# Mirrored rows read in 15 and 112 instead of 127, and the last batch's fold one MLP step later

## The chip, the cores and the metric

The kernel runs on one core of one Trainium2 chip. The metric is the device time of one execution in microseconds (us). Before the change three executions took 962.08, 965.52 and 968.96 us; their median is 965.52 us.

## The reference: what is computed

Three layers stand one behind the other, on 4 batches of 576 positions and 512 features.

```python
scores = scale * np.matmul(q, k.transpose(0, 1, 3, 2))     # 8 heads, local or strided mask
attn_out = softmax(masked scores) @ v                      # becomes x, [4, 576, 512]
...
X = np.fft.fft(np.fft.fft(x, axis=1), axis=2)
u = x + np.real(X)
un = (u - mean(u)) / np.sqrt(var(u) + 1e-06)
x = u + np.maximum(un @ w_ch1, 0.0) @ w_ch2                # first MLP, hidden width 2048
...
u = x + token_mlp(x)                                       # over the 576 positions
out = u + np.maximum(u @ w_ch1, 0.0) @ w_ch2               # second MLP, hidden width 1536
```

The change lies where the attention's result x of a batch is read for the Fourier layer.

## The kernel before, in words

**Stages.** Attention of the four batches comes first: per batch three groups of local heads and three of strided heads (matrix products `sc` for the scores, softmax on ScalarE, transposes `tp`, products `av`). The result `x` of each group is written to a DRAM buffer `xd[b]` (lines 270, 276, 277). The Fourier layer of batch b is worked off between the attention groups of later batches (`four[b]`), that of the last batch, `four[3]`, inside the first MLP. Then come the first MLP, the token layer and the second MLP.

**The Fourier layer of a batch.** The real part of a 2-D transform of real data is symmetric, so rows r and 576 - r are added first. `load(i)` (i = 0, 1, 2; 128, 128 and 33 rows) reads rows r0 and following of `xd[b]` into a tile `xa`, and the rows that mirror them into a tile `xr`; the second half of the positions is stored in reverse, so that the mirrored rows are consecutive too. For i = 0 row 0 has no mirror: row 0 of `xr` is set to zero on GpSimd, and the read brings rows 1 to 127, which are 127 rows of 2 KB (line 297). `prep(i)` (lines 299 to 316) folds on VectorE: `w` = xa + xr, then the two halves of `e`; ScalarE rounds `e` to `f` (line 315), GpSimd takes the rest (line 316). `s1(mt)`, five of them, multiplies `f` with the constants (products `g`, line 332), and ScalarE and VectorE split the result into `gh` and `gl` (lines 340, 342; `g4h`, `g4l` for the fifth). `s2(i)` multiplies these with further constants (products `fa`, `fb`, line 358), ScalarE copies `fa` to `sa`, VectorE forms `m` (lines 365, 366), adds it to `xa` and `xr` (line 371), and both are stored to `ud[b]` (lines 373, 374).

**The first MLP.** A step (c, f) takes one chunk c of 384 rows and one block f of 128 hidden units: 12 products `h` (line 411), the split of `h` into `hh` (ScalarE, line 415) and `hl` (VectorE, line 416), 9 products `oo` (line 430). `last_fft(x)` is called in the first nine steps and hands out the pieces of `four[3]`: the folds in steps 1 to 3, the `s1` in 3 to 5, the `s2` in 6 and 7, and in step 8 the memory of the Fourier constants is given to weights. Every step also begins to load one weight block: transfer `wraw` (line 101), four VectorE operations on `wu` (lines 108 to 113), `wAh` on ScalarE, `wAl` on GpSimd.

**What sets the order.** A scheduler orders the instructions of each engine at build time by its own model of time; `behind` gives it single orders (VectorE's fold behind an `hl` or a reduction `st`). On the chip each engine works through its list in that order, and an instruction that waits holds all behind it. SyncE (SP) issues all the transfers named here, in one list. Transfers that SP issues are given eight completion semaphores in turn, so a transfer can be issued only when the eighth before it has landed.

```python
self.last = nc.sync.dma_start(out=xr[z:n], in_=xd[self.b][287 + r0 + z:287 + r0 + n, :])
```

Of the kernel before, what the change touches and what calls it, by code (L numbers as in the profile page):

```python
# [43 lines left out]
def attention_fourier_mlp_kernel(ctx: ExitStack, tc: tile.TileContext, a: dict, out: bass.AP):  # L44
    nc = tc.nc
# [16 lines left out]
    xd = [dram.tile([S, DM], F32, name=f"xd{b}") for b in range(B)]  # L62
# [218 lines left out]
    class Fourier:  # L281
# [4 lines left out]
        def load(self, i):  # L286
            r0, n = ST[i]
            pool = self.pool if self.b % 2 else self.k["pool"]
            xa, xr = (pool.tile([P, DM], F32, tag=f"{x}{i}", name=x, bufs=1) for x in ("xa", "xr"))
            self.x[i] = xa, xr  # L290
            na, z = min(n, 288 - r0), 1 if i == 0 else 0
            if i == 2:
                nc.gpsimd.memset(xa[32:33], 0.0)
            if i == 0:
                nc.gpsimd.memset(xr[0:1], 0.0)
            nc.sync.dma_start(out=xa[:na], in_=xd[self.b][r0:r0 + na, :])
            self.last = nc.sync.dma_start(out=xr[z:n], in_=xd[self.b][287 + r0 + z:287 + r0 + n, :])

        def prep(self, i, prev=None, prev2=None):
            r0, n = ST[i]  # L300
# [187 lines left out]
    if True:  # L488
# [144 lines left out]
        def last_fft(x):  # L633
            nonlocal wb, wc
            x4 = four[3]
            prev = relu["hh"], relu["hl"]
            if 1 <= x < 4:
                x4.prep(x - 1, prev[1], prev[0])
            x4.after = prev
            for mt in {3: (0,), 4: (1, 2), 5: (3, 4)}.get(x, ()):  # L640
                x4.s1(mt)
            for i in {6: (0,), 7: (1, 2)}.get(x, ()):
                x4.s2(i)
            if x == 8:
                fst.close()
                wb = wbst.enter_context(tc.tile_pool(name="wb", bufs=16, side="left", reuse_waits="tile"))
                wc = wcst.enter_context(tc.tile_pool(name="wc", bufs=16, side="left", reuse_waits="tile"))
# [100 lines left out]
        def extra1(c, f):  # L748
            if steps.index((c, f)) <= 8:
                last_fft(steps.index((c, f)))  # L750
            advance()
            load_wa()
            if 2 <= c < NCH - 1 and f % 4 == 1:
                m, h = divmod((c - 2) * 4 + f // 4, 2)
                begin(blocks("2", m, 128 * h))
            if 2 <= c < NCH - 1 and f % 4 == 3:
                m, h = divmod((c - 2) * 4 + f // 4, 2)
                begin(blocks("1", m, 128 * h))
            if c == NCH - 1:
                if f >= 1:  # L760
                    load_wt()
                if f == 2:
                    c_load(0, range(3), 3)
                if f == 9:
                    c_load(1, range(5), 3)
# [458 lines left out]
```

## Time and profile before

| what | value |
|---|---|
| median of three executions | 965.52 us (962.08 to 968.96) |
| the profiled execution's own time | 963.61 us |
| its span, first to last instruction | 961.7 us |
| TensorE busy in the span | 900.6 us, 94% |
| VectorE, ScalarE, GpSimd busy | 559.4, 409.0, 307.7 us |
| mean granted TensorE clock | 0.976 of full |
| bytes moved by DMA | 160.99 MB, mean 167 GB/s |

The span is cut into views: what each engine waited for, the order of work on one engine (timeline), busy time in chosen stretches with the granted clock (1.00 is 2.4 GHz, 0.50 is 1.2 GHz) and the share of time in which the 16 DMA engines were busy, and the chain of work that ended last. "A <- B" in a wait says that A began when B ended. All rows are of the profiled execution, so sums are made against its 963.61 us.

### The profile page before, as it was taken

How to read it: one execution, taken by the hardware profiler on the slowest of the kernel's cores; microseconds unless marked ns; L12 is line 12 of the kernel's file. 1: busy time of each engine (PE TensorE's matmuls, PEld its weight loads, DVE VectorE, ACT ScalarE, POOL GpSimd, SP SyncE). 2: the span in 40 equal slices, each digit the busy share in tenths (PEclk: the TensorE clock that was granted, in tenths of full speed). 3: DMA queues.
4: the chain of work that ended last, by engine and by line, in shares of the span. 5: the costliest groups of instructions: out<-in, count | busy, mean ns of one | idle time of the engine just before them, and what ended most of it. 6: DMA issues, size and time to landing. Idle time of an engine off the chain costs nothing.

```text
span 961.7 us, 15392 instructions
## 1 busy us (share of the span) xinstructions
PE 900.6 (94%) x5554; PEld 830.6 (86%) x5554; DVE 559.4 (58%) x1046; ACT 409.0 (43%) x1069; POOL 307.7 (32%) x372
## 2 busy tenths in 40 slices
PE   7949688699999999999999999999999999999997
PEld 6949587589889899989788898777799999999997
DVE  4636677488999444343333344753725353989774
ACT  6948465345334224324222222521446454634441
POOL 4211212123333013434344344440430301746751
PEclk9979797999999999999999999999999999999999
DMA  9966654233443134465465565668943358344451
GB/s 253 270 206 200 201 175 149 94 124 113 137 134 108 66 111 136 125 190 152 141 186 151 150 208 161 181 209 284 351 166 153 129 184 278 89 149 164 171 197 45
DMA packets 116852, 160.99 MB, mean 167 GB/s; under 512 B 9543, under 2 KB 70061, under 8 KB 116777
## 3 DMA queue, kind: packets, MB, share of 16 engines
q1 hardware_dynamic: 114808, 157.29, 51.9%
q0 software_dynamic: 1712, 2.51, 1.0%
q8 instruction: 44, 0.72, 0.3%
q14 instruction: 32, 0.25, 0.1%
q10 hardware_dynamic: 256, 0.21, 0.1%
HBM read 104.92 MB, written 55.06 MB: 166 GB/s over the span
## 4 chain that ended last, share of the span: by engine, by line
PE 51%; DMA 19%; DVE 14%; SPq 5%; issue 4%; ACT 4%; POOL 4%; DVEq 0%; ACTq 0%; POOLq 0%
PE oo L1034 14%; PE z L893 8%; PE oo L430 6%; DMA xr<-xd 6%; PE h L411 5%; DMA wraw<-in_w1b_dram 5%; PE y L893 4%; SPq L101 3%; DMA xd<-x 3%; PE tu L804 3%; PE tk L782 3%; DVE wu L113 3%; DVE wu L112 3%; POOL wt L147 2%; DMA wraw<-in_w2b_dram 2%
## 5 line engine op out<-in xcount | busy, mean ns | idle before, releaser
L411 PE MATMUL h<-uT,wAh 128*128 128x384 f32 x768 | 203.0, 338 | 0.2
L411 PEld LDWEIGHTS h<-uT,wAh 128*128 128x128 f32 x768 | 139.1, 188 | 5.2 <-PE g L332 0.4
L1034 PE MATMUL oo<-wo,ht 128*128 128x256 f32 x972 | 133.7, 281 | 0.0
L411 PE MATMUL h<-uT,wAl 128*128 128x384 f32 x384 | 129.2, 336 | 0.0
L1034 PEld LDWEIGHTS oo<-wo,ht 128*128 128x128 f32 x972 | 126.5, 189 | 0.0
L430 PE MATMUL oo<-wAh,hh 128*128 128x512 f32 x288 | 114.2, 399 | 8.0 <-ACT hh L415 7.2
L430 PE MATMUL oo<-wAl,hh 128*128 128x512 f32 x288 | 113.6, 394 | 0.0
L430 PE MATMUL oo<-wAh,hl 128*128 128x512 f32 x288 | 105.3, 396 | 0.7 <-DVE hl L416 0.7
L416 DVE SCALAR_TENSOR_TENSOR hl<-h,hh 128x384 fp32r<-128x384 f32 x96 | 52.5, 552 | 74.9 <-ACT hh L415 74.9
L108 DVE TENSOR_SCALAR wu<-wu 128x512 f32<-128x512 f32 (+1 forms) x62 | 35.0, 565 | 85.5 <-ACT wu L106 79.4
L124 POOL TENSOR_TENSOR wAl<-wu,wAh 128x512 fp32r<-128x512 f32 x32 | 43.2, 1352 | 102.1 <-ACT wAh L123 100.7
L411 PEld LDWEIGHTS h<-uT,wAl 128*128 128x128 f32 x384 | 72.3, 188 | 3.0
L147 POOL TENSOR_TENSOR wt<-wu 128x128 f32<-128x128 f32 x48 | 21.1, 461 | 161.9 <-DVE wu L113 161.9
L106 ACT ACTIVATE wu<-wraw 128x512 f32<-128x512 f32 (+1 forms) x62 | 41.2, 664 | 72.8 <-DMA wraw<-in_w1b_dram 50.6
L430 PEld LDWEIGHTS oo<-wAh,hh 128*128 128x128 f32 x288 | 54.1, 188 | 20.4 <-ACT hh L415 9.8
L415 ACT ACTIVATE hh<-h 128x384 fp32r<-128x384 f32 x96 | 45.6, 481 | 53.2 <-PE h L411 50.8
L430 PEld LDWEIGHTS oo<-wAh,hl 128*128 128x128 f32 x288 | 53.6, 188 | 15.0 <-DVE hl L416 2.8
L893 PE MATMUL z<-ut,wo 128*128 128x384 f32 x324 | 64.5, 338 | 1.7 <-DVE ut L861 1.7
L210 PE MATMUL sc<-k,qz 128*96 128x128 f32 (+2 forms) x352 | 51.9, 288 | 14.7 <-DMA k<-in_kt_dram 14.7
L210 PEld LDWEIGHTS sc<-k,qz 128*96 128x96 f32 (+2 forms) x352 | 47.8, 186 | 18.0 <-issue 16.0
L430 PEld LDWEIGHTS oo<-wAl,hh 128*128 128x128 f32 x288 | 54.1, 188 | 8.8
L229 ACT ACTIVATE sm<-sc,st 96x128 f32<-96x128 f32 (+2 forms) x176 | 61.2, 368 | 0.6
(197 smaller groups left out, 1862.7 us busy)
## 6 DMA issues: line engine op xcount, KB each, us to landing
wo<-wsd SPq DMA_DIRECT2D x84, 256.0 KB
wsd<-wbh SPq DMA_DIRECT2D x24, 448.0 KB
wsd<-wbl SPq DMA_DIRECT2D x24, 448.0 KB
u<-u2d SPq DMA_DIRECT2D x36, 256.0 KB
hd<-hs SPq DMA_DIRECT2D x12, 768.0 KB
hw<-hd SPq DMA_DIRECT2D x36, 256.0 KB
wraw<-in_w1a_dram SPq DMA_DIRECT2D x16, 512.0 KB
wraw<-in_w2a_dram SPq DMA_DIRECT2D x16, 512.0 KB
```

Of the source, the lines that this page charges most:

```text
L106: behind(nc.scalar.activation(out=f32(u), in_=f32(high), func=AF.Abs, scale=2.0**16), relu.get("hh"))
L108: clamp = eng().tensor_scalar(f32(u), f32(u), E_MIN, E_MAX, op0=ALU.max, op1=ALU.min)
L124: nc.gpsimd.tensor_tensor(out=lo[:, :n], in0=u, in1=f32(hi[:, :n]), op=ALU.subtract)
L147: nc.gpsimd.tensor_tensor(out=o, in0=x, in1=y, op=ALU.add if plus else ALU.subtract)
L210: last = nc.tensor.matmul(out=sc[:q, j * k:(j + 1) * k], lhsT=qz[self.g][:, e, hp, qs], rhs=k_t[self.b, self.g][:, hp, ks], start=False, s ...
L229: self.exp = nc.scalar.activation(out=smv[:, j, :], in_=sc[:, j, :], func=AF.Exp, scale=SCALE, bias=st[:, 1, j:j + 1], accum_out=st[:, 2, ...
L411: nc.tensor.matmul(out=h[:, :384], lhsT=l[:, ws], rhs=r[:, kd, :], start=x == 0, stop=x == 11)
L415: relu["hh"] = nc.scalar.activation(out=hh, in_=h[:, :384], func=AF.Relu)
L416: relu["hl"] = nc.vector.scalar_tensor_tensor(out=hl, in0=h[:, :384], scalar=0.0, in1=f32(hh), op0=ALU.max, op1=ALU.subtract)
L430: nc.tensor.matmul(out=self.o[c][i], lhsT=l[:, s], rhs=r, start=first and x == 0, stop=last and x == 2)
L893: Unit.last = nc.tensor.matmul(out=bank[:, :384], lhsT=w[:, c + kd * P:c + kd * P + P], rhs=r[:, kd], start=first and x == 0, stop=x == 5, ...
L1034: nc.tensor.matmul(out=acc[G][bank][:, 256 * half:256 * half + 256], lhsT=lh[:, i], rhs=w[:, c:c + 256], start=m == 0 and x == 0 and half ...
```

## The change

The read of 127 mirrored rows becomes two transfers, of rows 1 to 15 (15 rows) and of rows 16 to 127 (112 rows). In the first MLP the last batch's folds are handed out in steps 2 to 4 instead of 1 to 3, its `s1` in 4 to 6 instead of 3 to 5, and its three `s2` all in step 7 instead of one in 6 and two in 7. Step 8 is as it was.

```diff
--- before.py
+++ after.py
@@ -288,13 +288,14 @@
             pool = self.pool if self.b % 2 else self.k["pool"]
             xa, xr = (pool.tile([P, DM], F32, tag=f"{x}{i}", name=x, bufs=1) for x in ("xa", "xr"))
             self.x[i] = xa, xr
-            na, z = min(n, 288 - r0), 1 if i == 0 else 0
+            na = min(n, 288 - r0)
             if i == 2:
                 nc.gpsimd.memset(xa[32:33], 0.0)
             if i == 0:
                 nc.gpsimd.memset(xr[0:1], 0.0)
             nc.sync.dma_start(out=xa[:na], in_=xd[self.b][r0:r0 + na, :])
-            self.last = nc.sync.dma_start(out=xr[z:n], in_=xd[self.b][287 + r0 + z:287 + r0 + n, :])
+            for c0, c1 in ([(1, 16), (16, n)] if i == 0 else [(0, n)]):
+                self.last = nc.sync.dma_start(out=xr[c0:c1], in_=xd[self.b][287 + r0 + c0:287 + r0 + c1, :])
 
         def prep(self, i, prev=None, prev2=None):
             r0, n = ST[i]
@@ -634,12 +635,12 @@
             nonlocal wb, wc
             x4 = four[3]
             prev = relu["hh"], relu["hl"]
-            if 1 <= x < 4:
-                x4.prep(x - 1, prev[1], prev[0])
+            if 2 <= x < 5:
+                x4.prep(x - 2, prev[1], prev[0])
             x4.after = prev
-            for mt in {3: (0,), 4: (1, 2), 5: (3, 4)}.get(x, ()):
+            for mt in {4: (0,), 5: (1, 2), 6: (3, 4)}.get(x, ()):
                 x4.s1(mt)
-            for i in {6: (0,), 7: (1, 2)}.get(x, ()):
+            for i in {7: (0, 1, 2)}.get(x, ()):
                 x4.s2(i)
             if x == 8:
                 fst.close()
```

On SP, where the first batch's rows are read (`xd_69` is batch 0's buffer, `xd_70` batch 1's; the later lines' numbers are one higher after the change):

```order
 L296 DMA xa<-xd_69 128x512
-L297 DMA xr<-xd_69 127x512
+L298 DMA xr<-xd_69 15x512
+L298 DMA xr<-xd_69 112x512
 L296 DMA xa<-xd_69 128x512
-L297 DMA xr<-xd_69 128x512
+L298 DMA xr<-xd_69 128x512
+L270 DMA xd_70<-x 96x2x256
 L296 DMA xa<-xd_69 32x512
-L270 DMA xd_70<-x 96x2x256
-L297 DMA xr<-xd_69 33x512
+L298 DMA xr<-xd_69 33x512
```

One transfer became two, and one store of batch 1 goes a place earlier. All transfers behind them take the next of the eight semaphores.

On VectorE, at the start of the first MLP, before the change (`hl` is the second MLP step's split, `w` the fold of `four[3]`, `gl` belongs to `four[2]`):

```order
L416 SCALAR_TENSOR_TENSOR hl<-h,hh 128x384
L310 TENSOR_TENSOR w<-xa,xr 128x510
L462 SCALAR_TENSOR_TENSOR mv<-nr,mv 128x3
L311 TENSOR_TENSOR e<-xa,xr 128x2
L108 TENSOR_SCALAR wu<-wu 128x512
L342 TENSOR_TENSOR gl<-g,gh 128x290
```

and after it:

```order
L417 SCALAR_TENSOR_TENSOR hl<-h,hh 128x384
L463 SCALAR_TENSOR_TENSOR mv<-nr,mv 128x3
L108 TENSOR_SCALAR wu<-wu 128x512
L477 SCALAR_TENSOR_TENSOR mv<-mv 128x3
L111 TENSOR_SCALAR wu<-wu 128x512
L343 TENSOR_TENSOR gl<-g,gh 128x290
L112 SCALAR_TENSOR_TENSOR wu<-wraw,wu 128x512
L113 SCALAR_TENSOR_TENSOR wu<-wraw,wu 128x512
L343 TENSOR_TENSOR gl<-g,gh 128x290
L417 SCALAR_TENSOR_TENSOR hl<-h,hh 128x384
L311 TENSOR_TENSOR w<-xa,xr 128x510
```

The fold stood ahead of the two `gl`; it now stands behind them and behind one more `hl`.

On VectorE, at the end of `four[3]`, before the change (from the second to the third `s2`):

```order
L365 TENSOR_TENSOR m<-sa,fb 128x258
L366 TENSOR_TENSOR m<-sa,fb 128x258
L113 SCALAR_TENSOR_TENSOR wu<-wraw,wu 128x512
L416 SCALAR_TENSOR_TENSOR hl<-h,hh 128x384
L371 TENSOR_TENSOR xa<-xa,m 128x512
L371 TENSOR_TENSOR xr<-xr,m 128x512
L108 TENSOR_SCALAR wu<-wu 128x512
L416 SCALAR_TENSOR_TENSOR hl<-h,hh 128x384
L111 TENSOR_SCALAR wu<-wu 128x512
L108 TENSOR_SCALAR wu<-wu 128x512
L112 SCALAR_TENSOR_TENSOR wu<-wraw,wu 128x512
L365 TENSOR_TENSOR m<-sa,fb 33x258
```

and after it:

```order
L366 TENSOR_TENSOR m<-sa,fb 128x258
L367 TENSOR_TENSOR m<-sa,fb 128x258
L372 TENSOR_TENSOR xa<-xa,m 128x512
L372 TENSOR_TENSOR xr<-xr,m 128x512
L417 SCALAR_TENSOR_TENSOR hl<-h,hh 128x384
L366 TENSOR_TENSOR m<-sa,fb 33x258
L367 TENSOR_TENSOR m<-sa,fb 33x258
```

Of the weight operations and `hl` between the two pieces one `hl` is left.

## Rows read from the trace of the kernel before

**Rows 1.** VectorE's waits, 0 to 265 us: us in total, times, longest.
```profile
DVE w L310 <- DMA xr<-xd: 37.3, 4, 11.5
```

**Rows 2.** TensorE's timeline: start us, us, instruction, [idle before <- releaser].
```profile
69.08 1.99 PE L210 MATMUL sc<-k,qz 128*96 128x128 f32 x8 [13.19 <-DMA k<-in_kt_dram]
...
107.46 0.58 PE L358 MATMUL fa<-alt,g4h 128*128 128x258 f32 x1 [9.08 <-ACT g4h L340]
...
155.84 0.64 PE L358 MATMUL fb<-sd,gh 128*33 128x258 f32 x2 [3.50 <-DVE m L366]
...
190.90 1.61 PE L332 MATMUL g<-cs,f 128*2 128x290 f32 x6 [6.89 <-DVE gl L342]
```

**Rows 3.** VectorE's timeline at the four folds, same columns.
```profile
63.63 0.69 DVE L310 TENSOR_TENSOR w<-xa,xr 128x510 f32<-128x510 f32 x1 [10.63 <-DMA xr<-xd]
...
104.45 0.69 DVE L310 TENSOR_TENSOR w<-xa,xr 128x510 f32<-128x510 f32 x1 [11.46 <-DMA xr<-xd]
...
153.04 0.69 DVE L310 TENSOR_TENSOR w<-xa,xr 128x510 f32<-128x510 f32 x1 [5.49 <-DMA xr<-xd]
...
189.30 0.69 DVE L310 TENSOR_TENSOR w<-xa,xr 128x510 f32<-128x510 f32 x1 [9.72 <-DMA xr<-xd]
```

**Rows 4.** Transfers in the chain that ended last: start us, us, transfer.
```profile
31.73 12.57 DMA xd<-x
...
48.03 15.47 DMA xr<-xd
...
63.52 5.42 DMA k<-in_kt_dram
...
139.04 13.88 DMA xr<-xd
...
172.41 2.20 DMA xd<-x
...
175.65 13.56 DMA xr<-xd
...
415.46 3.77 DMA x2d<-v
```

**Rows 5.** SP's timeline, 48 to 90 us: start us, us of issuing, transfer.
```profile
48.33 4.85 SPq L296 DMA_DIRECT2D xa<-xd  x1
...
56.26 1.17 SPq L175 DMA_DIRECT2D qz<-in_qt_dram  x2
63.52 0.36 SPq L176 DMA_DIRECT2D k<-in_kt_dram  x1
...
88.97 0.26 SPq L297 DMA_DIRECT2D xr<-xd  x1
89.28 3.86 SPq L296 DMA_DIRECT2D xa<-xd  x1
```

**Rows 6.** SP's waits, 0 to 260 us.
```profile
SPq L176 <- DMA xr<-xd: 6.1, 1, 6.1
```

**Rows 7.** Stretches: us, busy by engine (x instructions), TensorE's granted clock, DMA share, GB/s.
```profile
24.00:48.00 24.00, 23.79 (x234) 23.02 (x233) 14.59 (x36) 22.63 (x113) 4.81 (x9) 1.00 1.02 270
48.00:89.00 41.00, 27.76 (x244) 26.81 (x243) 23.64 (x54) 25.82 (x122) 6.66 (x6) 0.83 0.71 213
...
186.00:189.00 3.00, 0.00 (x0) 0.00 (x0) 0.00 (x0) 0.00 (x0) 0.00 (x0) 1.00 0.07 25
69.08:72.45 3.37, 3.37 (x15) 3.22 (x16) 1.34 (x5) 0.21 (x1) 0.29 (x1) 0.50 0.99 374
107.46:114.09 6.63, 6.63 (x31) 6.30 (x31) 6.60 (x16) 5.14 (x23) 1.78 (x2) 0.50 0.55 183
155.84:165.36 9.52, 8.68 (x42) 8.10 (x43) 9.52 (x19) 6.17 (x25) 4.78 (x4) 0.50 0.37 125
190.90:196.10 5.20, 5.20 (x23) 4.52 (x24) 4.87 (x12) 4.58 (x8) 1.04 (x1) 0.50 0.26 80
213.00:264.00 51.00, 50.18 (x285) 46.06 (x284) 47.01 (x83) 22.73 (x45) 15.95 (x11) 1.00 0.38 121
```

## The prediction

> **What bounds the kernel now.** I read the waits first, VectorE's before TensorE's. VectorE's longest wait is the fold `w` waiting for the transfer into `xr`: 37.3 us in four waits, one per batch [rows 1]. TensorE's timeline has four large holes, 13.19, 9.08, 3.50 and 6.89 us, together 32.7 us [rows 2]. Their releasers are a load of `k`, ScalarE's `g4h` and VectorE's `m` and `gl`, none of them `xr`; but each hole ends within 6 us of the moment at which VectorE gets its `xr` [rows 2, 3]. So VectorE is held at the head of its list by one transfer, and what TensorE needs stands behind the fold.
>
> Why is the transfer late? Where it was issued without a wait before it, it took 15.47, 13.88 and 13.56 us for 254 KB [rows 4], while a store of 256 KB landed in 3.77 us [rows 4]. From 186 to 189 us, deep in the last of these, no engine works and the DMA share is 0.07 [rows 7]: that is 1 of 16 engines (0.0625). The 127 rows go through one engine. It also holds the list of SP: the issue behind it takes 4.85 and 3.86 us where it otherwise takes around half a microsecond [rows 5], and `k` waits 6.1 us for `xr`, which is the eighth transfer before it [rows 6].
>
> After each hole TensorE's granted clock is 0.50 (1.2 of 2.4 GHz) for a while, with 3.37, 6.63, 8.68 and 5.20 us of work in those stretches [rows 7]. At full clock this work would take about half.
>
> From 213 us TensorE is busy 50.18 of 51 us [rows 7], and so it stays to the end but for small waits: what is gained before 200 us is passed on whole.
>
> **The split of the read.** Removed: four transfers of 127 rows. Added: eight, of 15 and 112 rows, so four more issues on SP at 0.26 us each (the issue of `xr`) [rows 5], 1 us in all, beside engines that work. What 15 or 112 rows take no row shows. Bounds: below, 2.20 us, a store of 63 KB [rows 4]; above, 15.47 us, as before. I take 3.77 us, the row nearest in size; the gain is the same up to about 4 us.
>
> Batch 0. VectorE is free at 63.63 - 10.63 = 53.00 us [rows 3], and `xr` issued by 48.3 would land at 52.1. TensorE's hole, from 55.9 to 69.08, ends with `k`, issued at 63.52 and landed 5.42 us later [rows 2, 4, 5]. The two `qz` ahead of it were issued by 57.43; with the 4.85 us issue cut to half a microsecond, and 0.3 us for the added transfer, they are out by 53.4 and `k` follows at once, since its eighth predecessor is then the 112-row read, landed by 52.1. So `k` lands at 58.8: 10.1 us earlier. Half of 3.37 us at low clock is 1.7. Gain 11.8.
>
> Batch 1. Issue at 88.97 + 0.26, landing at 93.0; VectorE is free at 104.45 - 11.46 = 92.99. VectorE gains 11.46. TensorE could gain 9.08 + 6.63/2 = 12.4, but then waits for VectorE, which is busy 6.60 of 6.63 us behind the hole [rows 7]. Gain: the smaller, 11.5.
>
> Batch 2. Landing at 139.3 + 3.8 = 143.1; VectorE is free at 147.55. VectorE gains 5.5, TensorE could gain 3.50 + 8.68/2 = 7.8. VectorE is busy 9.52 of 9.52 us in the stretch behind [rows 7], so 5.5.
>
> Batch 3. Landing at 175.9 + 3.8 = 179.7; VectorE is free at 179.58. VectorE gains 9.7, TensorE 6.89 + 5.20/2 = 9.5. Gain 9.5.
>
> Sum 38.3 us.
>
> **What is late next.** The transfers themselves. Between the first and the second read of `xr`, 48 to 89 us, the DMA engines are busy 0.71 of 41 us, which is 29.1 us of full use [rows 7]; with batch 0's 11.8 us gone the stretch is 29.2 us long. It becomes as full as 24 to 48 us, where the share is 1.02 [rows 7] and where a store `xd` took 12.57 us to land against 2.20 later [rows 4]. `xr` of batch 1 can only be read behind its `xd`, and VectorE has no slack there (93.0 against 92.99). This costs between nothing and 12.57 - 2.20 = 10.4 us; I take the middle, 5. Net of the split: 33.3 us.
>
> **A rule that speaks against it.** The row is the DMA share of 0.07, one engine at work while fifteen rest [rows 7]. The Trainium skill, "DMA: Bandwidth & Descriptors", Rules for kernel authors, says of two transfers to disjoint partition halves not to bother: they use the same engines and come one behind the other. By that alone the split would gain nothing and the time would stay at 963.6. It speaks of transfers that already use all 16; the row shows that this one does not. The same page, Why a DMA increments its semaphore by 16 and not by 1, says that the number of engines is the largest divisor up to 16 of the outer row count: 1 for 127, which the row bears out, 15 for 15 and 16 for 112, which no run here shows yet.
>
> **The last batch a step later.** No instruction is added. The fold of `four[3]` moves behind two `gl` of `four[2]`. In the kernel before this is the fourth hole's cause; once `xr` lands at 179.7, the fold would wait some 0.1 us where it stood, so the move adds at most that to the 9.5. At the far end three `s2` share one step. Their VectorE work now has one `hl` between the second and third where there were two and five weight operations: less TensorE work lies between a product `fb` and the one that needs its bank again. A wait there costs between 0 and 3.50 us (the same wait in batch 2 [rows 2]), twice: 0 to 7; in the other direction the moved fold may spare 1. I take 0, since TensorE is hardly waiting in this stretch. What covers the later folds is VectorE's own slack, 4 of 51 us from 213 on [rows 7].
>
> **Sum.** 963.6 - 33.3 = 930.3 us of a profiled execution. The median is 1.9 us above it (965.52 against 963.61), so 932 us.
>
> **Rivals.**
> - *The queue takes over.* Every batch's read waits for a store `xd` that lands late in a full queue. For: the full stretch above. Against: from 89 us on there is room, and in batch 2 VectorE has 4.4 us in hand. Price: 10.4 us in batch 1, some 6 (10.4 less 4.4) in batch 2, and 2 for `k`, 18 of the 38.3: a gain of 20, about 945 us.
> - *The split does not spread.* The 112 rows go through one engine as the 127 did: 112/127 of 13.56 us is 12.0, 1.6 us saved four times, less the waits of 15 more rows behind: at most 6 us, about 960, within 1%. Against: 3.77 us for 128 rows.
> - *Slower: the stacked second stage.* The three `s2` in step 7 each make TensorE wait as in batch 2 (3.50 us) and drop to the low clock behind it, where 8.68 us of work lost 4.3: 3 x 7.8 = 23.5 us. It decides only where the split gains less than that; with the rival above, 963.6 - 6 + 23.5 + 1.9 gives 983. For: VectorE is busy 47.01 of 51 us there [rows 7]. Against: TensorE has `h` and `oo` products of other steps between them.
>
> **How the numbers follow.** The forecast has 0.82, the queue 0.12, the split that does not spread 0.04, the slower one 0.02. The low end of the range has no loss to the queue and the batches' TensorE gains in full (batch 1 one us more, batch 2 two): 963.6 - 41.3, about 922, and a little lower, 921. The high end takes in the queue rival: 947. A change of under 1% (9.7 us) is about what a measurement of this kernel cannot tell from none: faster 0.94, same 0.04, slower 0.02.
>
> **What would show it.** Right: VectorE's wait of `w` for `xr` falls from 37.3 us to under 8; TensorE's holes with their four releasers shrink to some 3 us in batch 0 and under 3 elsewhere; `k` of batch 2 is issued near 53 us; no issue of 4 us stands behind `xr`; the low clock behind the holes is mostly gone; the first MLP's even part begins some 33 us earlier. Queue term: the share between the first two reads rises towards 1, and a wait of `w` for `xr`, or of SP for `xd`, is left in batch 1. Wrong, if transfers of 15 or 112 rows take over 8 us, if new holes stand between the attention groups that end with `qz`, `k` or `xd`, or if `fb` waits for `m` in the first MLP by more than 3 us.

## The result and the profile after

| | before | after |
|---|---|---|
| median | 966.88 us (962.08 to 968.96, 4 runs) | 926.79 us (925.19 to 928.16, 4 runs) |
| ratio after to before | | 0.9592, 95% interval 0.9549 to 0.9635 |
| the profiled execution's own time | 963.61 us | 925.51 us |
| its span | 961.7 us | 923.7 us |
| mean granted TensorE clock | 0.976 | 0.995 |

The median before is that of the three executions named above and a fourth. The change took 40.1 us off the median and 38.1 us off the profiled execution. The forecast was 932 us, with a range from 921 to 947.

VectorE's waits for the read, from 0 to 265 us of the kernel after, which answer to [rows 1] (columns as there):

```profile
DVE w L311 <- DMA xr<-xd: 2.1, 2, 1.1
```

37.3 us in four waits have become 2.1 in two: batches 2 and 3 no longer wait at the fold at all. Their places, in VectorE's timeline of the kernel after, one line for each of the four first folds as in [rows 3]:

```profile
53.42 0.69 DVE L311 TENSOR_TENSOR w<-xa,xr 128x510 f32<-128x510 f32 x1 [1.09 <-DMA xr<-xd]
...
85.26 0.69 DVE L311 TENSOR_TENSOR w<-xa,xr 128x510 f32<-128x510 f32 x1 [1.01 <-DMA xr<-xd]
...
128.36 0.68 DVE L311 TENSOR_TENSOR w<-xa,xr 128x510 f32<-128x510 f32 x1
...
157.07 0.68 DVE L311 TENSOR_TENSOR w<-xa,xr 128x510 f32<-128x510 f32 x1
```

TensorE's timeline of the kernel after, its largest holes between 50 and 265 us, against the four of [rows 2]:

```profile
60.46 1.99 PE L210 MATMUL sc<-k,qz 128*96 128x128 f32 x8 [5.24 <-DMA k<-in_kt_dram]
...
91.96 0.39 PE L359 MATMUL fa<-alt,g4l 128*128 128x258 f32 x1 [1.25 <-DVE g4l L343]
...
120.38 0.96 PE L333 MATMUL g<-cs,f 128*2 128x290 f32 x6 [2.65 <-DVE gl L343]
```

The hole at `k` went from 13.19 to 5.24 us, the one at `fa` from 9.08 to 1.25; the holes at `fb` (3.50) and in the first MLP (6.89) are gone. The 2.65 us are not new: in the kernel before TensorE stood still for 2.50 us ahead of the same product, at 139.50 us.

SP's timeline in the kernel after, at the first batch's reads, which answers to [rows 5]:

```profile
47.35 0.78 SPq L298 DMA_DIRECT2D xr<-xd  x2
48.17 0.41 SPq L296 DMA_DIRECT2D xa<-xd  x1
...
53.61 0.57 SPq L176 DMA_DIRECT2D k<-in_kt_dram  x1
```

The issue behind the mirrored rows takes 0.41 instead of 4.85 us, and `k` is issued at 53.61 instead of 63.52 us. In the chain of work that ended last, transfers of the kernel after:

```profile
47.75 5.55 DMA xr<-xd
...
56.45 8.72 DMA xd<-x
```

The 112 rows landed after 5.55 us, in the place of 15.47 [rows 4]. The stretches of the kernel after that answer to [rows 7], columns as there:

```profile
47.40:80.80 33.40, 28.11 (x249) 27.15 (x247) 24.06 (x55) 26.03 (x122) 7.07 (x6) 0.90 0.88 260
80.80:120.50 39.70, 35.61 (x314) 33.82 (x313) 33.77 (x80) 28.42 (x123) 10.02 (x8) 1.00 0.82 247
213.00:264.00 51.00, 51.00 (x269) 46.35 (x268) 44.93 (x76) 21.50 (x38) 16.69 (x12) 1.00 0.39 127
60.46:64.00 3.54, 3.54 (x16) 3.39 (x17) 1.49 (x5) 0.21 (x1) 0.00 (x0) 0.50 1.03 415
```

Between the first two reads of `xr` the same work now fits into 33.40 us instead of 41.00, and the DMA share rose from 0.71 to 0.88. The clock is still halved behind the hole at `k`, and in this execution behind no other hole.

Where the time was gained is read from one instruction that stands in both traces, VectorE's `x` of the attention (its count is given), and the first `tk` of the token layer:

| marker | before, us | after, us | shift | gained in this step | forecast |
|---|---|---|---|---|---|
| 9th `x`, ahead of batch 0's fold | 52.02 | 51.35 | 0.7 | 0.7 | 0 |
| 14th `x` (batch 0) | 88.50 | 80.14 | 8.4 | 7.7 | 11.8 |
| 19th `x` (batch 1) | 139.37 | 120.25 | 19.1 | 10.8 | 11.5 |
| 24th `x` (batch 2) | 171.40 | 144.97 | 26.4 | 7.3 | 5.5 |
| first `tk` (batch 3) | 618.12 | 580.37 | 37.8 | 11.3 | 9.5 |
| end of the span | 961.7 | 923.7 | 38.0 | 0.2 | 0 |

The forecast column sums to 38.3; a term of 5 for the queue was taken off it. The 0.7 us ahead of the first read are not the split's: experiment 2, which leaves the split out, has the 9th `x` at 51.18 us.

### The profile page after: what moved, and what is told of

It reads as the page before. It is cut to its first block, busy times and chain, and to the rows that moved or that the text cites. A ratio compares the mean times of both kernels' runs of the same rounds, so it can differ in the third digit from the quotient of the medians.

```text
span 923.7 us, 15401 instructions
## 1 busy us (share of the span) xinstructions
PE 891.2 (96%) x5554; PEld 822.6 (89%) x5554; DVE 556.0 (60%) x1046; ACT 409.0 (44%) x1069; POOL 311.2 (34%) x372
## 4 chain that ended last, share of the span: by engine, by line
PE 56%; DMA 14%; DVE 13%; ACT 4%; SPq 4%; POOL 4%; issue 3%; DVEq 0%; ACTq 0%; POOLq 0%
PE oo L1035 14%; PE oo L431 8%; PE h L412 8%; PE z L894 8%; DMA wraw<-in_w1b_dram 5%; PE y L894 4%; SPq L101 3%; PE tu L805 3%; PE tk L783 3%; POOL wt L147 3%; DMA xd<-x 3%; DVE wu L112 2%; DMA wraw<-in_w2b_dram 2%; PE w L894 2%; DVE wu L113 2%
## 5 line engine op out<-in xcount | busy, mean ns | idle before, releaser
L124 POOL TENSOR_TENSOR wAl<-wu,wAh 128x512 fp32r<-128x512 f32 x32 | 45.8, 1434 | 103.9 <-ACT wAh L123 93.7
L894 PEld LDWEIGHTS z<-ut,wo 128*128 128x128 f32 x324 | 56.4, 188 | 2.1 <-DVE ut L862 2.1
```

The costliest lines, as they stand in the source:

```text
L124: nc.gpsimd.tensor_tensor(out=lo[:, :n], in0=u, in1=f32(hi[:, :n]), op=ALU.subtract)
L894: Unit.last = nc.tensor.matmul(out=bank[:, :384], lhsT=w[:, c + kd * P:c + kd * P + P], rhs=r[:, kd], start=first and x == 0, stop=x == 5, ...
```

## The experiments

The kernel before, run beside them on the same chip, took 965.21 us (experiments 1 to 4), 964.06 (5, 9, 10) and 964.03 (6 to 8).

**1. The split alone.** The last batch's pieces stay in their old steps.

```diff
-            if 2 <= x < 5:
-                x4.prep(x - 2, prev[1], prev[0])
+            if 1 <= x < 4:
+                x4.prep(x - 1, prev[1], prev[0])
...
-            for mt in {4: (0,), 5: (1, 2), 6: (3, 4)}.get(x, ()):
+            for mt in {3: (0,), 4: (1, 2), 5: (3, 4)}.get(x, ()):
...
-            for i in {7: (0, 1, 2)}.get(x, ()):
+            for i in {6: (0,), 7: (1, 2)}.get(x, ()):
```

> The split of the read alone; the last batch's pieces stay in the steps of the kernel before. Theory 1 (the one-engine transfer is the whole cause): 925 to 930 us, VectorE's waits of w for xr under 4 us, the four TensorE holes as after the change, the fourth (6.89 us) gone as well. Rival (the fourth hole is taken away by the later step, not by the split): the fourth hole stays at 4 us or more and the time is 933 to 938 us.

Measured: 928.46 us (927.25 to 931.34), ratio 0.9627 (0.9595 to 0.9659). VectorE's fold waits for `xr` 3.1 us in three waits. The fourth fold, where it stood before, in VectorE's timeline of this run:

```profile
155.20 0.69 DVE L311 TENSOR_TENSOR w<-xa,xr 128x510 f32<-128x510 f32 x1 [0.84 <-DMA xr<-xd]
```

What follows: nearly all of the gain is the split's. Left in its old step, the fold of the last batch waits 0.84 us instead of 9.72 [rows 3].

**2. The move alone.** One read of 127 rows, the pieces of the last batch in their new steps.

```diff
-            for c0, c1 in ([(1, 16), (16, n)] if i == 0 else [(0, n)]):
+            for c0, c1 in ([(1, n)] if i == 0 else [(0, n)]):
```

> The later step alone; the read of 127 rows stays one transfer. Theory 1: the first three batches as before, VectorE waits for xr some 25 us or more in the first three folds; the fourth wait is cut by what the fold stands later; 956 to 964 us. Rival (the move does nothing by itself): 964 to 969 us. Rival (the move costs in the first MLP): over 969 us and waits of fb for m there.

Measured: 960.23 us (957.62 to 961.90), ratio 0.9943 (0.9912 to 0.9974). VectorE's timeline of this run at the fourth fold, and TensorE's at the hole behind it:

```profile
192.29 0.69 DVE L311 TENSOR_TENSOR w<-xa,xr 128x510 f32<-128x510 f32 x1 [7.59 <-DMA xr<-xd]
```

```profile
194.81 0.58 PE L359 MATMUL fa<-alt,g4l 128*128 128x258 f32 x1 [6.40 <-DVE g4l L343]
```

What follows: the move takes the hole from `gl` and gives it, hardly smaller (6.40 against 6.89 us), to the next instruction that needs VectorE, `g4l`, which in the kernel before had stood for 0.94 us of its own. VectorE's waits for `xr` are 37.9 us in total, as long as before. Without the split the move saves 2.4 us by the first `tk` of the profile; by the medians 5.0, with an interval from 2.5 to 8.5. It couldn't remove the wait, only hand it on.

**3 and 4. The same cut in other places.** 14 and 113 rows; 5 and 122 rows. 113 is prime, 122 is 2 x 61.

```diff
-            for c0, c1 in ([(1, 16), (16, n)] if i == 0 else [(0, n)]):
+            for c0, c1 in ([(1, 15), (15, n)] if i == 0 else [(0, n)]):
```

```diff
-            for c0, c1 in ([(1, 16), (16, n)] if i == 0 else [(0, n)]):
+            for c0, c1 in ([(1, 6), (6, n)] if i == 0 else [(0, n)]):
```

> The changed kernel, but the 127 rows are cut into 14 and 113; 113 is prime. Theory 1 (what counts is over how many DMA engines the rows divide): the 113 rows go through one engine, 113/127 of 13.5 us is 12.0 us, so VectorE waits 20 us or more for xr and the time is 953 to 963 us. Rival (any cut of the read in two helps, by shorter pieces or by the shifted semaphores): 925 to 930 us.

> The changed kernel, but the 127 rows are cut into 5 and 122; 122 is 2 x 61. Theory 1: two engines with 61 rows each, 61/127 of 13.5 us is 6.5 us, with a microsecond or two in front 6.5 to 8.5 us to land: VectorE waits 5 to 14 us for xr, 931 to 943 us, between the changed kernel and the cut of 14 and 113. Rival (any cut helps alike): 925 to 930 us. Rival (anything but a full spread is as slow as one engine): 953 us or more.

Measured: 954.99 us (952.34 to 959.23) with 113 rows, 940.63 us (938.98 to 940.98) with 122. In the chain that ended last, reads of `xr` with 113 rows:

```profile
47.87 13.48 DMA xr<-xd
...
87.67 14.34 DMA xr<-xd
...
171.11 12.95 DMA xr<-xd
```

and with 122 rows:

```profile
47.03 11.41 DMA xr<-xd
...
86.28 9.89 DMA xr<-xd
```

Late in the last batch's read of `xr`, when little else is under way, the stretches with 113 rows (first view) and with 122 (second view), columns as in [rows 7]:

```profile
182.00:184.00 2.00, 1.43 (x11) 1.16 (x10) 0.00 (x0) 0.00 (x0) 0.00 (x0) 1.00 0.07 25
```

```profile
168.50:170.50 2.00, 2.00 (x15) 2.00 (x14) 1.97 (x6) 2.00 (x4) 0.00 (x0) 1.00 0.13 49
```

What follows: 113 rows, one more than 112, take almost as long as 127 did (13.56 to 15.47 us [rows 4]), while the larger piece of 122 rows is faster. Neither the number of pieces nor their size decides, but the row count. These two views count the engines: a share of 0.07 is one of 16 (0.0625), as with 127 rows [rows 7], and 0.13 with about twice the GB/s is two of 16 (0.125); with 122 rows SP had issued nothing since 166.1 us. Both times fell into the range of theory 1, but the sizes in it were too small: 122 rows took 9.89 and 11.41 us in the chain, where 6.5 to 8.5 were expected, and the idle time ahead of the four first folds was 14.8 us, where the upper bound was 14.

**5. One row and 126.** 126 is 14 x 9 and not a multiple of 16.

```diff
-            for c0, c1 in ([(1, 16), (16, n)] if i == 0 else [(0, n)]):
+            for c0, c1 in ([(1, 2), (2, n)] if i == 0 else [(0, n)]):
```

> The changed kernel with the 127 rows cut as 1 and 126 instead of 15 and 112. Theory (a transfer is spread over the largest divisor of its row count up to 16): 126 rows go over 14 engines, so xr lands in about 4 us, w waits under 4 us in total, 925 to 930 us. Rival (only counts that 16 divides spread, or only small ones): 126 rows behave nearly like 127 or 113, w waits 24 to 37 us in total, 950 to 963 us.

Measured: 926.93 us (925.42 to 928.41), the time of the change itself. VectorE's waits of this run, 0 to 265 us, and the reads of `xr` in its chain:

```profile
DVE w L311 <- DMA xr<-xd: 3.9, 2, 2.2
```

```profile
47.76 6.90 DMA xr<-xd
...
82.59 4.55 DMA xr<-xd
```

What follows: a transfer of only one row less than before takes 6.90 and 4.55 us (about 4 were expected) where 127 rows took 13.56 to 15.47 [rows 4]. The times stand in the order of the largest divisor up to 16 (1 for 127 and 113, 2 for 122, 14 for 126, 16 for 112), and so does the idle time ahead of the four first folds, whatever releaser the view names: 37.3, 28.8, 14.8, 3.9 and 2.1 us. Only for one and two engines does a view count them.

**6. `k` second.** The remaining hole of 5.24 us ends with `k`. Here SP issues the `qz` and `k` of batch 2 behind the first reads of `xa` and `xr` of batch 0 and ahead of the others.

```diff
...
                 for i in range(3):
-                    four[b - 1].load(i)
+                    four[b - 1].load(i, first if i else None)
+                    if i == 0:
+                        first = load_qk(2, 0, ap, four[0].last) if b == 1 else None
...
-                load_qk(b + 1, 0, ap)
+                if b != 1:
+                    load_qk(b + 1, 0, ap)
...
```

The lines left out let `load` and `load_qk` take and return the transfer behind which the next is ordered.

> The changed kernel with one thing different: SyncE issues batch 2's loads of qz and k right behind the first two reads of xr (15 and 112 rows) of batch 0, ahead of the other reads of that batch. What is left of the first hole is 5.24 us of TensorE waiting for k, issued at 53.6 us and landed at 60.3, and some 3.5 us of work at the low clock behind it. Theory (the hole is only the place of k in SyncE's list): k is issued near 49.5 and lands near 55 to 56, the hole falls to under 1 us, the low clock behind it goes, and the gain of 4 to 6 us is passed on: 921 to 924 us. Rival (the stretch is bound by the transfers themselves, 0.90 of the DMA engines' time): k lands earlier, but the reads that now stand behind it, or the store xd of batch 1, land as much later, and VectorE's waits of w for xr rise by 3 us or more in batch 0 or 1: 925 to 928 us.

Measured: 924.19 us (919.63 to 926.41), ratio 0.9567 (0.9542 to 0.9592). TensorE's hole in its timeline:

```profile
57.65 1.08 PE L211 MATMUL sc<-k,qz 128*96 128x128 f32 x8 [2.30 <-DMA k<-in_kt_dram]
```

and VectorE's first two folds of batch 0:

```profile
53.49 0.69 DVE L312 TENSOR_TENSOR w<-xa,xr 128x510 f32<-128x510 f32 x1 [1.04 <-DMA xr<-xd]
...
59.91 0.69 DVE L312 TENSOR_TENSOR w<-xa,xr 128x510 f32<-128x510 f32 x1 [4.70 <-DMA xr<-xd]
```

What follows: by its mechanism this is the rival, though the time lies between the two ranges. The hole at `k` shrank by 2.9 us, and the second fold, which did not wait before, now waits 4.70. The share of the DMA engines' time in this stretch of the changed kernel is 0.88; the 0.90 of the expectation is TensorE's clock in the same row. At the 14th `x` (80.32 us) this run is no earlier than the change (80.14). By the median it is 2.6 us below the change, but the two intervals of the ratio overlap; whether it is faster is not settled.

**7. `k` first.** `qz` and `k` ahead of all reads of batch 0.

```diff
...
             if gi == 2 and b > 0:
+                first = load_qk(2, 0, ap) if b == 1 else None
                 for i in range(3):
-                    four[b - 1].load(i)
+                    four[b - 1].load(i, first)
...
```

> As the run before, but qz and k stand ahead of all of batch 0's reads, so that xr is read last. Theory: k lands near 53 and the hole at k goes; xr lands some 4 us later, so VectorE's w waits about 4 us, of which part is passed on through g4h and fa: 924 to 928 us, no better than the run before. Rival: VectorE's 1.1 us wait today shows that xr and VectorE are level, and what stands behind w is needed late enough that 4 us don't matter: 921 to 923 us.

Measured: 928.11 us (921.81 to 931.49), ratio 0.9606 (0.9570 to 0.9642). The first fold waits 6.95 us for `xr`, the second batch's 3.29, and the hole at `k` is 1.55 us. What follows: no better than the change, as the theory had it, at a price of 7 us where it said 4. From 48 to 60 us of the changed kernel the DMA share is 0.99, and in both runs a shorter wait for `k` came with a longer one for `xr`: the transfers fill this stretch, and their order chooses who waits.

**8. `k` first, in the kernel before.** The same order with the one read of 127 rows.

> The kernel before (one read of 127 rows) with qz and k of batch 2 issued ahead of batch 0's reads. It tells what the releaser of the first hole, k, was worth by itself: 13.19 us of idle time and 1.7 us of low clock. Theory (two chains end at the same place: k behind xr in SyncE's list, and VectorE held at the fold by xr, with the reductions and splits that TensorE needs behind it): k lands near 53, but VectorE waits for xr to 64 to 68 us and TensorE waits for VectorE instead, so the hole keeps 8 to 15 us under another releaser: 960 to 968 us. Rival (k alone): the hole goes and VectorE catches up beside full TensorE work: 952 to 956 us.

Measured: 965.73 us (962.93 to 968.18), ratio 1.0012 (0.9993 to 1.0031). TensorE's timeline of this run, and VectorE's at the fold:

```profile
58.42 1.09 PE L211 MATMUL sc<-k,qz 128*96 128x128 f32 x8 [1.43 <-DMA k<-in_kt_dram]
...
72.85 0.85 PE L333 MATMUL g<-cs,f 128*128 128x290 f32 x2 [12.24 <-ACT f L316]
```

```profile
70.41 0.69 DVE L311 TENSOR_TENSOR w<-xa,xr 128x510 f32<-128x510 f32 x1 [17.09 <-DMA xr<-xd]
```

and the read in its chain:

```profile
50.20 20.09 DMA xr<-xd
```

What follows: `k` is the releaser that the trace names for a hole of 13.19 us [rows 2], and in this order freeing it is worth nothing: the hole comes back as 12.24 us under ScalarE's `f`, which needs the fold. Two chains ended at the same place, and both began at the transfer of `xr`. The run is not a clean price of `k`, though: behind `qz` and `k` the read of `xr` was issued later and took 20.09 instead of 15.47 us, so that it landed 6.8 us later than before (70.29 against 63.50). What an early `k` is worth beside an `xr` that lands as before was not tried. SP's issue behind that transfer took 9.85 us in this run.

**9 and 10. The change and the split alone, once more side by side.** The edits are none and that of experiment 1.

> The changed kernel once more, beside the next run on the same chip, to price the later fold of the last batch beside the split. Theory (the move is worth what the positions in the profiles show, 1.6 us): 1 to 3 us below the next run. Rival (nothing that can be told): the two within 1 us of each other.

> The split alone, with the last batch's pieces in their old steps, once more beside the run before. Theory: 1 to 3 us above the run before, about 928 us. Rival: within 1 us of it. In both, its last fold waits under 1 us for xr.

Measured: 925.97 us (923.57 to 927.00) with the move, 928.56 us (928.08 to 932.54) without; ratios 0.9598 (0.9574 to 0.9622) and 0.9643 (0.9617 to 0.9668). The first pair, which did not run side by side, had 926.79 against 928.46. What follows: 2.6 and 1.7 us in favour of the move, both times of one sign. The intervals of the two ratios just overlap, but every execution without the move (928.08 us or more) is slower than every one with it (927.00 or less) in the pair that ran side by side. The last fold waited 1.61 us in experiment 10, where under 1 was expected.

## Why the prediction was right

**What bounds the kernel.** That one transfer on one engine held VectorE's list, SP's list and, through both, TensorE was the right reading. Experiments 3 to 5 show it against the reading by size, and the DMA shares of 0.07 and 0.13 against the reading by pieces. Experiment 8 speaks against the reading by releasers alone, with the reservation made there. The Trainium skill, "DMA: Bandwidth & Descriptors", Why a DMA increments its semaphore by 16 and not by 1, gives the number of engines as the largest divisor up to 16 of the outer row count; the five row counts agree in the order of their times, and the shares count one engine for 127 and 113 rows and two for 122; 14 and 16 are counted by no row. The advice in its Rules for kernel authors not to split into partition halves rests on halves that spread over all 16 engines; it does not carry over to a whole that has no such divisor: here the split alone gave some 36 us (928.46 against 965.21, 928.56 against 964.06).

**The split, batch by batch.** Of the marks named for it, `w` waits 2.1 us (under 8), `k` is issued at 53.61 (near 53), no issue of 4 us stands behind the read, and the holes of batches 1 to 3 are under 3 us; only the first hole is larger, 5.24 where some 3 were named. The sizes of the steps were off in both directions:

- Batch 0, forecast 11.8, measured 7.7. `k` was issued when the forecast said (53.61, forecast 53.4), but from there to TensorE's start it took 6.85 us (60.46), 1.3 more than the 5.56 before (69.08 - 63.52 [rows 2, 5]). So 5.24 us of hole were left instead of some 3, and the clock fell behind it as before (0.50 for 3.54 us of work), so its 1.7 us were not won back. The 1.3 and 1.7 us, the 0.2 by which `k` was issued late and the 0.7 counted ahead of the first read make up 3.9 of the 4.1 us that are missing.
- Batch 1, forecast 11.5, measured 10.8. The 112 rows took about 4.0 us (from the middle of the paired issue, 81.2, to 85.26), near the 3.77 that was taken. A wait of 1.01 us is left, and SP waits 4.4 us for the store `xd` ahead of this read (3.4 before), as the queue term said it would be, but far under its bound of 10.4.
- Batch 2, forecast 5.5, measured 7.3 here and 6.0 in the second profile of the same kernel (experiment 9, same markers). TensorE's own figure was 7.8. The step took the smaller of two engines' gains because VectorE was busy all through the stretch behind the hole; the measured gain lies between the two.
- Batch 3, forecast 9.5: the split alone gave 10.0 and 8.5 in its two profiles (shift of the first `tk` less that of the 24th `x`: 36.1 - 26.1 and 35.0 - 26.5), the change 11.3 and 11.5 (37.75 - 26.43 and 36.2 - 24.7).

**The queue term of 5.** Batches 0 and 1 together fell 4.8 us short (4.1 + 0.7), close to the 5 that was taken, and the share between the reads rose to 0.88. It did not go where the term had it, though: VectorE's wait in batch 1 is 1 us, and what was lost in batch 0 is `k` and the clock behind it. That the amount fits is luck in part: it is the middle between nothing and 10.4 us, which were worked out for another place. Experiments 6 and 7 show the same stretch again: `k` earlier makes `xr` later. The total came out 4.8 us better than forecast (925.5 against 930.3 in the profile) because batches 2 and 3 brought 3.6 us more, 0.7 was gained ahead of the first read and 0.2 behind the last marker. Two slips in the working changed little: the store that landed in 2.20 us [rows 4] is one of 54 KB and not 63, and the low end of the range, 963.6 - 41.3, lacks the 1.9 us from the profiled execution to the median, with which it is 924.

**The move.** It was priced at 0, with 0.1 in batch 3, up to 1 for it and up to 7 against it. The bound against it was empty: TensorE waits for no `m` in the first MLP. In its favour the forecast fell short. By the positions it is worth 1.3 to 3 us (11.3 and 11.5 against 10.0 and 8.5), by the two pairs of medians 1.7 and 2.6. The positions carry the clock too: in experiment 1 it is 0.57 from 148 to 152 us, where the change has 1.00, which by itself is about 1.7 us (an estimate, 0.43 of 4 us), more than the 1.3 between that pair. In the pair of experiments 9 and 10 both have one such stretch, and there the difference is 3.0. What it takes away is seen in TensorE's waits of the second split-alone run, 100 to 265 us, which the change does not have:

```profile
PE fa L359 <- DVE g4l L343: 1.9, 1, 1.9
...
PE oo L431 <- DVE u L435: 0.7, 1, 0.7
```

The forecast priced the wait of the fold alone (0.1; measured 0.84 and 1.61) and not that the fold's own instructions keep VectorE from `four[2]`'s `gl` and `g4l` even where nothing is late. That this explains all of the 2 us was not tried, and the intervals of the ratios leave room for less.

**The rivals.** The split that does not spread is what 113 rows look like (955 us); with 112 it does not occur. Of the queue that takes over, batch 1's wait of 1.01 us is there, against a price of 10.4. The stacked second stage did not appear.

## What to carry to other kernels

Look at the row count of every transfer that stands alone at the head of an engine's list: a count without a large divisor up to 16, like 127, took two to three times as long here as its neighbour 126, and it also held the list that issued it. Name the cause of a hole only when both lists that end there are followed back: here the releaser that the trace named was freed, and nothing was gained. Once such a stall is gone, ask whether the transfers fill the stretch (a share of 0.99 here): then reordering them moves the wait instead of removing it.

## What was not expected of the hardware

The same kernel in two profiled executions had TensorE's clock at full speed or at half behind one hole. In the first the hole at `gl` was 2.65 us long, in the second 3.05. TensorE's timeline and the stretches in the second execution:

```profile
120.87 1.30 PE L333 MATMUL g<-cs,f 128*2 128x290 f32 x6 [3.05 <-DVE gl L343]
...
147.66 0.54 PE L333 MATMUL g<-cs,f 128*128 128x290 f32 x2 [0.98 <-POOL f L317]
```

```profile
120.50:124.50 4.00, 3.63 (x19) 3.15 (x19) 3.60 (x17) 3.34 (x17) 0.00 (x0) 0.60 0.61 177
148.00:152.00 4.00, 3.89 (x13) 3.30 (x12) 3.93 (x11) 0.72 (x2) 0.00 (x0) 0.57 0.35 112
```

and in the first:

```profile
120.40:124.50 4.10, 4.10 (x38) 3.81 (x39) 3.85 (x17) 3.32 (x16) 0.00 (x0) 1.00 0.71 195
148.00:152.00 4.00, 4.00 (x26) 4.00 (x25) 3.72 (x16) 1.13 (x3) 0.00 (x0) 1.00 0.47 150
```

That is 19 recorded products against 38 in about the same time. In the second execution the clock also fell near 148 us, behind a wait of only 0.98 us; the first has the same wait, 1.00 us at 145.93 us, and kept its clock. So a part of what a removed hole gives back through the clock is not certain from one execution to the next. It fits that batch 2's step gave 7.3 us in one profile and 6.0 in the other: the stretch from 120.5 us lies in that step, and 4 us at 0.60 are about 1.6 us of full clock (an estimate). The one near 148 us lies in batch 3's.

An issue on SP behind the read of 127 rows took 4.85 and 3.86 us [rows 5], 4.02 us in batch 2 and 9.85 us in experiment 8, against 0.41 behind the 112 rows and 0.36 to 0.65 behind 122: the cost of such a transfer is not only its own time. Behind 113 rows it took 2.62 and 3.50 us in the first two batches; in the third it took 0.47, and the one after it 2.65. What holds the issue is not shown.
